# Loading a corner of the query weights with sixteen small loads on few DMA engines, in an attention decode kernel

## The chip, the cores and the metric

The kernel runs on one core of a Trainium2 chip. The core has a matrix engine (TensorE, PE in the profile), a vector engine (VectorE, DVE), an activation engine (ScalarE, ACT), a general engine (GpSimd, POOL), a queue engine that here only issues loads and the store (SyncE, SP), and 16 DMA engines that move data between the chip's memory and the core's on-chip memory of 128 partitions. The metric is the device time of one execution in microseconds, as the median of several runs. Lower is better.

## What is computed

One token of attention for 32 sequences: a query projection, attention over the last 512 positions of a key and value cache with 8 key heads shared by 32 query heads, and an output projection. Everything is bf16.

```
x: [32, 1, 512]   k_cache, v_cache: [32, 8, 2048, 128]
wq: [512, 4096]   wo: [4096, 512]     W = 512, rep = 4
q = (x @ wq).reshape(B, Sq, 32, 128).transpose(0, 2, 1, 3)
k = repeat(k_cache[:, :, Sk - W:, :], rep, axis=1)
v = repeat(v_cache[:, :, Sk - W:, :], rep, axis=1)
p = softmax(einsum("bhqd,bhkd->bhqk", q, k) * Dh ** -0.5)
o = einsum("bhqk,bhkd->bhqd", p, v)
out = o.transpose(0, 2, 1, 3).reshape(B, Sq, 4096) @ wo
```

The windows of the two caches are 33.6 MB each, wq and wo 4.2 MB each.

## The kernel before

**Start.** ACT issues four small loads of x, with 2, 6, 10 and 14 of its 32 rows (`X_PARTS`, L187). SP issues two loads of wq. Row 4p + k of wq goes to partition p, slice k (k = 0 to 3), so that a partition's four rows are contiguous in memory; load 0 brings slices 0 and 1, load 1 slices 2 and 3, 16 KB in each partition each time (`load_wq`, L193). Load 0 is issued before the block of engine programs, load 1 is the first instruction of SP's program. They use the buffer `V_sb[1]`, which later holds values.

**Query projection.** PE transposes x with four matmuls into the PSUM bank `Y_ps` (L301), DVE casts the result into `xT_sb` (L413). Then PE runs, for each slice k and each of eight column groups n of 512 columns, one matmul of `xT_sb[:, k]` with the slice's columns into PSUM bank n (L313): 32 matmuls, accumulated over k. When slice 3 is done for a group, the semaphore `pe_q` goes up. DVE copies the even groups and ACT the odd ones into `Q_row` (L434, L490). DVE transposes that into `QT_sb` (L437), and POOL spreads it into the block-diagonal `QBD`.

**The loop.** Eight steps q take four sequences each. For each, K and V are loaded into one of two buffers (4 MB a load; the V loads of steps 5, 6 and 7 come in two halves), DVE transposes K in two halves (`turn`, T, L445), PE computes scores (S, L331), ACT exponentiates, DVE normalizes, PE moves the probabilities to the layout of the value rows (E, L346), ACT and DVE spread them into the buffer `bd` (B), and PE multiplies them by V (P, L361). The results are picked out of PSUM (C), folded by matmuls with an identity (F, L373) and put away in `o_sel` (D). PE's, DVE's and ACT's orders of these operations are written out by hand at the top of the file, as is SP's order of loads:

```
K0 K1 V0.0 K2 V1.0 K3 V2.0 K4 V3.0 K5 K6 V4.0 K7 V5.0 V5.1 V6.0 V6.1 V7.0 V7.1 W0 W1 W2
```

SP issues a K load (L228) once DVE has transposed what is in the buffer, a V load (L236) once PE has consumed it (V1 waits for `pe_q` at 8, since it overwrites wq), and the three pieces of wo (W0, W1, W2: 2048, 1536 and 512 KB, L242) once the last but one K is transposed; they go into the K buffer.

**End.** PE multiplies `o_sel` with each piece of wo as it lands (L393), DVE and ACT copy the result out of PSUM in two steps, and SP stores it (L248).

**A buffer with two lives.** `bd` holds two halves. The first use of its half 0 is the spreading of step 0; its half 1 also holds x, the identities and `xT_sb` at the start.

Of the kernel before, what the change touches and what calls it, by code (L numbers as in the profile page):

```python
# [6 lines left out]
F32 = mybir.dt.float32  # L7
ACTF = mybir.ActivationFunctionType
# [30 lines left out]
X_PARTS = [(0, 2), (2, 8), (8, 18), (18, 32)]  # L39
V_PIECES = [1, 1, 1, 1, 1, 2, 2, 2]  # L40
WOP = [(0, 16), (16, 28), (28, 32)]


def ops_of(text):
# [3 lines left out]
def bass_standalone__sliding_block_cached__sampling_kernel(  # L48
# [10 lines left out]
    HD = wq.shape[1]  # L59
# [60 lines left out]
    with ExitStack() as es:  # L120
# [23 lines left out]
        junk = sb("junk", [P, 2], F32)  # L144

        wq_sb = V_sb[1][:, :].rearrange("p (kt n) -> p kt n", kt=DKT)
        wo_sb = K_sb[0][:, :].rearrange("p (i n) -> p i n", i=NI)


# [11 lines left out]

        ps = es.enter_context(nc.psum_tensor("ps", [P, 8, 512], F32))
        S_ps, EP_ps, O_ps, F_ps, Y_ps = ps[:, 0], ps[:, 1], ps[:, 2:6], ps[:, 6], ps[:, 7]

        sem_x = sem("sem_x")
        sem_wq = [sem(f"sem_wq{i}") for i in range(DKT // 2)]
        sem_k = [sem(f"sem_k{i}") for i in range(2)]
        sem_v = [[sem(f"sem_v{i}_{j}") for j in range(max(V_PIECES))] for i in range(2)]
        sem_wo = [sem(f"sem_wo{i}") for i in range(len(WOP))]
        sem_out = sem("sem_out")  # L170
        names = (
            "pe_xT pe_q pe_Y dve_xT dve_q dve_QT dve_m dve_r dve_y dve_c act_q act_y act_warm "
            "pool_x pool_e pool_ei pool_q pool_f pool_m pool_j pool_qbd pool_fz"
        ).split()
        s = {n: sem(n) for n in names}
# [14 lines left out]

        def load_wq(i):

            nc.sync.dma_start(  # L193
                wq_sb[:, 2 * i:2 * i + 2, :].rearrange("p k n -> p (k n)"),
                wq.rearrange("(p k) n -> p k n", k=DKT)[:, 2 * i:2 * i + 2].rearrange("p k n -> p (k n)"),
            ).then_inc(sem_wq[i], 16)

        load_wq(0)
# [19 lines left out]
        @block.sync  # L218
        def _(sp):
            wait = Waits(sp)  # L220
            load_wq(1)
            wo_r = wo.rearrange("(p i) n -> p i n", i=NI)
            for op in ops_of(" ".join(LOADS)):
                kind, q = op[0], op[1]
                if kind == "K":
                    if q >= 2:
                        wait([ends["T", q - 2, 1]])
                    sp.dma_start(K_sb[q % 2][:, :], rows(k_cache, q)).then_inc(sem_k[q % 2], 16)  # L228
                elif kind == "V":
                    if q == 1:  # L230
                        sp.wait_ge(s["pe_q"], 8)
                    if q >= 2:
                        wait([ends["P", q - 2, 31]])
                    n = R // V_PIECES[q]
                    r0 = op[2] * n
                    sp.dma_start(  # L236
                        V_sb[q % 2][:, r0 * DH:(r0 + n) * DH], rows(v_cache, q, r0, r0 + n)
                    ).then_inc(sem_v[q % 2][op[2]], 16)
                else:
                    wait([ends["T", NQ - 2, 1]])  # L240
                    i0, i1 = WOP[q]
                    sp.dma_start(  # L242
                        wo_sb[:, i0:i1, :].rearrange("p i n -> p (i n)"),
                        wo_r[:, i0:i1, :].rearrange("p i n -> p (i n)"),
                    ).then_inc(sem_wo[q], 16)
            sp.wait_ge(s["dve_y"], 2)
            sp.wait_ge(s["act_y"], 2)
            sp.dma_start(  # L248
                out.rearrange("b s n -> b (s n)"), out_sb[:, :, :].rearrange("b c n -> b (c n)")
            ).then_inc(sem_out, 16)  # L250
            sp.wait_ge(sem_out, 16)
# [44 lines left out]
        def _(pe):  # L296
# [3 lines left out]
            for kt in range(DKT):  # L300
# [4 lines left out]
                    start=True, stop=True, tile_position=(0, 0),  # L305
                )
            ins.then_inc(s["pe_xT"], 1)
            pe.wait_ge(s["dve_xT"], 1)
            for kt in range(DKT):
                if kt % 2 == 0:  # L310
                    pe.wait_ge(sem_wq[kt // 2], 16)
                for n in range(8):
                    ins = pe.matmul(  # L313
                        ps[:, n], lhsT=xT_sb[:, kt, :], rhs=wq_sb[:, kt, n * 512:(n + 1) * 512],
                        start=kt == 0, stop=kt == DKT - 1, tile_position=(0, 0),
                    )
                    if kt == DKT - 1:
                        ins.then_inc(s["pe_q"], 1)

            def scores(q, w):  # L320
                if w == 0:
# [87 lines left out]
        @block.vector  # L409
        def _(dve):  # L410
            wait = Waits(dve)
            dve.wait_ge(s["pe_xT"], 1)
            dve.tensor_copy(  # L413
                xT_sb[:, :, :].rearrange("p k c -> p (k c)"), Y_ps
            ).then_inc(s["dve_xT"], 1)
            dve.wait_ge(s["pool_f"], 2)
            dve.tensor_reduce(
                F_hd[:, :], F_id[:, :, :].rearrange("p r h -> p h r"), AX.X, ALU.add
            ).then_inc(s["dve_c"], 1)
            dve.wait_ge(s["pool_m"], 2)  # L420
            dve.tensor_reduce(
                m_red[:, :].rearrange("p (h k) -> p h k", h=HKV),
                m_id[:, :, :, :].rearrange("p b h k -> p h k b"), AX.X, ALU.add,
            ).then_inc(s["dve_c"], 1)
            dve.wait_ge(s["dve_c"], 2)
            dve.wait_ge(s["pool_fz"], 1)
            dve.tensor_reduce(
                mask[:, :], m_red[:, :].rearrange("p (h k) -> p h k", h=HKV), AX.X, ALU.add
            ).then_inc(s["dve_c"], 1)
            for d in range(4):  # L430
                dve.tensor_copy(F_sb[:, d, :, d], F_hd[:, :]).then_inc(s["dve_c"], 1)
            for n in range(4):
                dve.wait_ge(s["pe_q"], 2 * n + 1)
                dve.tensor_copy(Q_row[:, 1024 * n:1024 * n + 512], ps[:, 2 * n]).then_inc(s["dve_q"], 1)  # L434
            dve.wait_ge(s["dve_q"], 4)
            dve.wait_ge(s["act_q"], 4)
            dve.transpose(  # L437
                QT_sb[:, :, :, :, :].bitcast(F32).rearrange("p j w h t -> p h w (j t)"),
                Q_row.bitcast(F32).rearrange("p (h w c) -> p h w c", h=HQ, w=2),
            ).then_inc(s["dve_QT"], 1)  # L440
            dve.wait_ge(s["dve_QT"], 1)

            def turn(q, w):
                dve.wait_ge(sem_k[q % 2], 16 * (q // 2 + 1))
                return dve.transpose(  # L445
                    KT_sb[:, w].bitcast(F32).rearrange("p r c t -> p r (c t)"),
                    K_sb[q % 2][:, :].bitcast(F32).rearrange("p (r w c) -> p r w c", r=R, w=2)[:, :, w],
                )

            def maxes(q):  # L450
                dve.tensor_reduce(maxv[:, q:q + 1], S_ps, AX.X, ALU.max).then_inc(s["dve_m"], 1)  # L451
                dve.wait_ge(s["dve_m"], q + 1)
                return dve.tensor_scalar(  # L453
                    negmax[:, q:q + 1], maxv[:, q:q + 1], -SCALE, None, op0=ALU.mult)

            def norm(q):
                dve.reciprocal(recip[:, q:q + 1], sums[:, q:q + 1]).then_inc(s["dve_r"], 1)
                dve.wait_ge(s["dve_r"], q + 1)
                return dve.tensor_scalar(  # L459
                    P_bf[:, :], P_f32[:, :], recip[:, q:q + 1], None, op0=ALU.mult)  # L460

            def spread(q, h0, h1):
                for h in range(h0, h1):
                    o, i, m = spread_args(q, h)
                    ins = dve.tensor_scalar(o, i, m, None, op0=ALU.mult)  # L465
                return ins

            def pick(q, r0, r1):
                for r in range(r0, r1):
                    ins = dve.tensor_copy(*pick_args(q, r))  # L470
                return ins

            run = {"T": turn, "M": maxes, "N": norm, "B": spread, "C": pick}
            for op in orders["DVE"]:
                wait(needs(op))
                run[op[0]](*op[1:]).then_inc(op_sem["DVE", op[0]], 1)
            for c in (0, 2):
                dve.wait_ge(s["pe_Y"], c // 2 + 1)
                dve.tensor_copy(  # L479
                    out_sb[:, c, :], Y_ps[32 * c:32 * (c + 1), 0:P]  # L480
                ).then_inc(s["dve_y"], 1)

        @block.scalar
        def _(act):
            wait = Waits(act)
            act.wait_ge(s["pool_j"], 1)
            act.activation(junk[:, 1:2], junk[:, 0:1], ACTF.Exp).then_inc(s["act_warm"], 1)
            for n in range(4):
                act.wait_ge(s["pe_q"], 2 * n + 2)
                act.activation(  # L490
                    Q_row[:, 1024 * n + 512:1024 * n + 1024], ps[:, 2 * n + 1], ACTF.Copy
                ).then_inc(s["act_q"], 1)
# [66 lines left out]
```

## Time and profile before

| what | value |
|---|---|
| time, median of 3 runs | 186.34 us (186.14 to 186.37) |
| the profiled execution's own time | 186.56 us |
| its span, first to last instruction | 184.7 us |
| mean granted TensorE clock | 0.823 |
| PE, DVE, ACT, POOL busy | 65%, 58%, 27%, 9% of the span |
| DMA: bytes, mean rate | 75.80 MB, 410 GB/s |
| share of the chain of waits that is DMA | 77% |
| issue of the K0 load by SP | 1.65 us |
| x transposes on PE (L301) | from 9.20 us |
| wq matmuls on PE (L313), 32 of them | from 10.57 us, 8.51 us |
| Q transpose on DVE (L437) | 20.13 us, 3.62 us |
| first K transposes on DVE (L445) | from 23.78 us |
| last wo load issued / last PE work on it | 157.99 / 181.68 us |

The span is shorter than the time by what lies before the first and behind the last instruction. Times inside the execution are counted from the span's start. A load's landing is told by a semaphore that each DMA engine involved raises once its share has arrived, so the trace holds up to 16 landing events for a load. The trace also holds a record of every packet that a DMA engine moved, with its queue (q1 is SP's, q10 is ACT's, q8 and q14 bring instructions), start, duration and size, but not the number of the engine.

### The profile page before, as it was taken

Reading aid. Unit: us, or ns where it says so; the run is one execution under the profiler, and the core shown is the slowest. Engines: PE = TensorE matmul, PEld = TensorE weight load, DVE = VectorE, ACT = ScalarE, POOL = GpSimd, SP = SyncE. Lnnn points to the kernel's source line nnn. Section 1 sums busy time; section 2 is a strip of 40 time slices with the busy share of each in tenths; the row PEclk is TensorE's granted clock in tenths of the full one; section 3 lists DMA queues with packets and bytes.
Section 4 is the critical chain, followed back from the end, with each engine's and each line's share of the span. In section 5 each row is a group of like instructions: output and inputs, shape, how many; then the busy total and the mean of one; then the engine's idle time right before and its main releaser. Section 6 shows DMA issues by size and latency. Waiting matters only on the chain.

```text
span 184.7 us, 3662 instructions
## 1 busy us (share of the span) xinstructions
PE 119.1 (65%) x1636; PEld 56.8 (31%) x1636; DVE 106.6 (58%) x106; ACT 49.8 (27%) x93; POOL 16.9 (9%) x52
## 2 busy tenths in 40 slices
PE   0089104447696795549944992441799899888872
PEld 0034000014452351304431350000345445444362
DVE  0031999994549631973299327999646996302031
ACT  3001300011935157001650162001062704502031
POOL 7900040202000200002000200020000000000000
PEclk9999955555599999657987699555579999999999
DMA  6999999999999999999999999999999999999970
GB/s 217 415 490 390 426 454 454 433 390 426 451 447 429 405 422 447 440 436 397 421 451 447 433 397 426 447 440 426 419 429 405 426 426 422 440 412 429 423 299 30
DMA packets 3584, 75.80 MB, mean 410 GB/s; under 512 B 432, under 2 KB 496, under 8 KB 624
## 3 DMA queue, kind: packets, MB, share of 16 engines
q1 hardware_dynamic: 3504, 75.53, 95.9%
q8 instruction: 13, 0.21, 0.5%
q10 hardware_dynamic: 64, 0.03, 0.1%
q14 instruction: 3, 0.02, 0.0%
HBM read 75.53 MB, written 0.03 MB: 409 GB/s over the span
## 4 chain that ended last, share of the span: by engine, by line
DMA 77%; DVE 13%; issue 3%; PE 3%; SPq 3%; DVEq 0%
DMA K_sb<-in_k_cache_dram 49%; DMA V_sb<-in_v_cache_dram 15%; DMA K_sb<-in_wo_dram 13%; DVE KT_sb L445 12%; PE ps L361 2%; SPq L236 1%; SPq L228 1%; SPq L242 1%; PE ps L331 1%; SPq L193 0%; DVE C_sb L470 0%; DVE maxv L451 0%; PE ps L393 0%; DVEq L120 0%; DVE P_bf L479 0%
## 5 line engine op out<-in xcount | busy, mean ns | idle before, releaser
L445 DVE STREAM_TRANSPOSE KT_sb<-K_sb 128x4096 f32<-128x4096 f32 x16 | 70.6, 4433 | 12.5 <-DMA K_sb<-in_k_cache_dram 12.4
L361 PE MATMUL ps<-V_sb,bd 32*128 32x512 bf16 x1024 | 63.1, 397 | 4.7 <-DMA V_sb<-in_v_cache_dram 2.9
L331 PE MATMUL ps<-KT_sb,QBD 128*32 128x512 bf16 x256 | 25.3, 532 | 39.7 <-DVE KT_sb L445 30.0
L361 PEld LDWEIGHTS ps<-V_sb,bd 32*128 32x128 bf16 x1024 | 27.0, 97 | 38.1 <-issue 12.3
L331 PEld LDWEIGHTS ps<-KT_sb,QBD 128*32 128x32 bf16 x256 | 6.6, 114 | 56.1 <-DVE KT_sb L445 37.0
L496 ACT ACTIVATE P_f<-ps,negmax 128x512 f32<-128x512 f32 x8 | 5.5, 687 | 63.1 <-DVE negmax L453 63.1
L509 ACT ACTIVATE bd<-PTc,mask 128x512 bf16<-128x512 bf16 x31 | 20.1, 710 | 0.3
L514 ACT ACTIVATE C_sb<-ps 32x512 f32<-32x512 f32 x22 | 12.9, 587 | 25.6 <-PE ps L361 25.4
L289 POOL COPY QBD<-QT_sb 32x128 bf16<-32x128 bf16 x32 | 9.2, 287 | 106.6 <-PE ps L331 90.2
L465 DVE TENSOR_SCALAR bd<-PTc,mask 128x512 bf16<-128x512 bf16 x33 | 9.3, 348 | 13.8 <-ACT PTc L503 13.8
L470 DVE COPY C_sb<-ps 32x512 f32<-32x512 f32 x10 | 6.9, 693 | 15.7 <-PE ps L361 15.6
L373 PE MATMUL ps<-C_sb,F_sb 128*128 128x128 f32 x64 | 10.0, 303 | 6.3 <-ACT C_sb L514 5.7
L346 PE MATMUL ps<-P_bf,E_sb 128*128 128x128 bf16 x128 | 11.0, 255 | 0.8 <-DVE P_bf L459 0.8
L373 PEld LDWEIGHTS ps<-C_sb,F_sb 128*128 128x128 f32 x64 | 8.3, 203 | 9.3 <-ACT C_sb L514 8.0
L346 PEld LDWEIGHTS ps<-P_bf,E_sb 128*128 128x128 bf16 x128 | 9.3, 116 | 4.9 <-DVE P_bf L459 2.8
L451 DVE TENSOR_REDUCE maxv<-ps 128x1 f32<-128x512 f32 x8 | 5.5, 686 | 7.3 <-PE ps L331 7.2
L503 ACT ACTIVATE PTc<-ps 128x512 bf16<-128x512 f32 x8 | 4.8, 594 | 18.2 <-PE ps L346 18.0
L313 PE MATMUL ps<-V_sb,bd 128*128 128x512 bf16 x32 | 8.5, 433 | 0.8 <-DVE bd L413 0.8
L301 PE MATMUL ps<-bd 32*128 32x128 bf16 x4 | 0.6, 296 | 9.2 <-DMA bd<-in_x_dram 9.2
L413 DVE CAST bd<-ps 128x512 bf16<-128x512 f32 x1 | 0.7, 692 | 9.8 <-PE ps L301 9.8
L434 DVE CAST KT_sb<-ps 128x512 bf16<-128x512 f32 x4 | 2.5, 684 | 6.0 <-PE ps L313 6.0
L490 ACT ACTIVATE KT_sb<-ps 128x512 bf16<-128x512 f32 x4 | 2.1, 603 | 14.0 <-PE ps L313 14.0
(29 smaller groups left out, 33.9 us busy)
## 6 DMA issues: line engine op xcount, KB each, us to landing
K_sb<-in_k_cache_dram SPq DMA_DIRECT2D x8, 4096.0 KB, 25.7
V_sb<-in_v_cache_dram SPq DMA_DIRECT2D x5, 4096.0 KB, 30.1
V_sb<-in_v_cache_dram SPq DMA_DIRECT2D x6, 2048.0 KB, 16.5
V_sb<-in_wq_dram SPq DMA_DIRECT2D x2, 2048.0 KB, 10.0
K_sb<-in_wo_dram SPq DMA_DIRECT2D x1, 2048.0 KB, 19.9
K_sb<-in_wo_dram SPq DMA_DIRECT2D x1, 1536.0 KB, 22.9
K_sb<-in_wo_dram SPq DMA_DIRECT2D x1, 512.0 KB, 23.6
out_dram<-P_bf SPq DMA_DIRECT2D x1, 32.0 KB, 1.5
```

What stands on the lines that cost most here:

```text
L289: pool.tensor_copy(QBD[pr, q % 2].rearrange("p (w t) (h c) -> p w t h c", w=2, h=HKV)[:, :, :, :, 4 * b:4 * b + 4], QT_sb[pr, q].rearrange ...
L313: ins = pe.matmul(ps[:, n], lhsT=xT_sb[:, kt, :], rhs=wq_sb[:, kt, n * 512:(n + 1) * 512], start=kt == 0, stop=kt == DKT - 1, tile_positio ...
L331: ins = pe.matmul(S_ps[32 * c:32 * c + 32, :], lhsT=QBD[:, q % 2, 2 * w + t, c0:c0 + 32], rhs=KT_sb[:, w, :, KB * h:KB * h + KB, t], start ...
L346: ins = pe.matmul(EP_ps[:, e * R:(e + 1) * R], lhsT=E_sb[:, k, e].rearrange("p m j -> p (m j)"), rhs=P_bf[:, k * R:(k + 1) * R], start=k = ...
L361: ins = pe.matmul(O_ps[:, b, :], lhsT=bd[pr, q % 2, 4 * g:4 * g + 4].rearrange("p r h e -> p (r h e)"), rhs=V_sb[q % 2][pr, 512 * g:512 * ...
L373: ins = pe.matmul(F_ps[:, 0:P], lhsT=F_sb[:, d].rearrange("p h d -> p (h d)"), rhs=C_sb[:, q % 2, :, 32 * d:32 * d + 32], start=d == 0, st ...
L445: return dve.transpose(KT_sb[:, w].bitcast(F32).rearrange("p r c t -> p r (c t)"), K_sb[q % 2][:, :].bitcast(F32).rearrange("p (r w c) -> ...
L451: dve.tensor_reduce(maxv[:, q:q + 1], S_ps, AX.X, ALU.max).then_inc(s["dve_m"], 1)
L465: ins = dve.tensor_scalar(o, i, m, None, op0=ALU.mult)
L470: ins = dve.tensor_copy(*pick_args(q, r))
L509: ins = act.activation(o, i, ACTF.Copy, scale=m)
L514: ins = act.activation(*pick_args(q, r), ACTF.Copy)
```

## The change

The second wq load brings slice 2 in full and only the first 3072 columns of slice 3: 14 KB in each partition instead of 16. The cut-off corner, 1024 columns of the 128 rows 4j + 3, is loaded by 16 new loads. Each takes rows of 2 KB, one or two for each of e partitions (e = 3, 5 or 6, four partitions apart), into 48 partitions of half 0 of `bd`, in three slots. Four loads have e = 3 (one row each, j from 0), four e = 5 (one row, j from 12), eight e = 6 (two rows, j from 32 and 56). SP issues them behind the second wq load and ahead of K0, after it has waited for a DVE memset that clears the area (rows of the slots that no load fills must be zero).

The x columns that belong to these rows are transposed separately: six more small matmuls on PE behind the four, copied by DVE (two copies, slots 0 and 1) and ACT (two copies, slot 2) into `xTx_sb`, also in `bd`. They use parts of PSUM banks 5 and 6, so PE waits for the ACT copies before group 5 of slice 0 and for the DVE copies before group 6. In slice 3, PE runs groups 0 to 5 as before; groups 6 and 7 are closed by three matmuls each, one for each slot over 64 partitions, after a wait for all 16 loads.

```diff
+WQX = [(0, 3, 32, 1), (12, 5, 0, 1), (32, 6, 0, 2), (56, 6, 32, 2)]
+WQX_AT = {3: (0,), 5: (12,), 6: (32, 56)}
+NX = 6
...
         def load_wq(i):

+            n = 2 * HD - i * (HD - 512 * NX)
             nc.sync.dma_start(
-                wq_sb[:, 2 * i:2 * i + 2, :].rearrange("p k n -> p (k n)"),
-                wq.rearrange("(p k) n -> p k n", k=DKT)[:, 2 * i:2 * i + 2].rearrange("p k n -> p (k n)"),
+                wq_sb[:, 2 * i:2 * i + 2, :].rearrange("p k n -> p (k n)")[:, 0:n],
+                wq.rearrange("(p k) n -> p k n", k=DKT)[:, 2 * i:2 * i + 2].rearrange(
+                    "p k n -> p (k n)")[:, 0:n],
             ).then_inc(sem_wq[i], 16)
...
             load_wq(1)
+            sp.wait_ge(s["dve_wqx"], 1)
+
+            for j0, e, p0, slots in WQX:
+                t = 4 * e * len(WQX_AT[e])
+                rows_x = wq.rearrange("(j k) n -> j k n", k=DKT)[
+                    WQX_AT[e][0]:WQX_AT[e][0] + t * slots, DKT - 1, 512 * NX:].rearrange(
+                        "(s t) n -> t s n", t=t)
+                for r in range(4):
+                    j = j0 - WQX_AT[e][0] + r
+                    s0 = 0 if slots == 2 else 2
+                    sp.dma_start(
+                        wqx_sb[p0 + r:p0 + r + 4 * e - 3:4, s0:s0 + slots, :], rows_x[j:j + 4 * e - 3:4]
+                    ).then_inc(sem_wqx, 16)
...
             ins.then_inc(s["pe_xT"], 1)
+            x_last = x_sb.rearrange("b (j k) -> b k j", k=DKT)[:, DKT - 1]
+            for j0, e, p0, slots in WQX:
+                for i in range(slots):
+                    slot = i if slots == 2 else 2
+                    ins = pe.matmul(
+                        XT_ps[slot][p0:p0 + 4 * e],
+                        lhsT=x_last[:, j0 + 48 * i:j0 + 48 * i + 4 * e],
+                        rhs=xsel[:, :, :].rearrange("p a j -> p (a j)"),
+                        start=True, stop=True, tile_position=(0, p0),
+                    )
+            ins.then_inc(s["pe_xTx"], 1)
...
-                for n in range(8):
+                for n in range(8 if kt < DKT - 1 else NX):
+                    if kt == 0 and n == NX - 1:
+                        pe.wait_ge(s["act_xT"], 2)
+                    if kt == 0 and n == NX:
+                        pe.wait_ge(s["dve_xT"], 3)
...
+            pe.wait_ge(sem_wqx, 16 * 4 * len(WQX))
+            for n in range(NX, 8):
+                for slot in range(3):
+                    ins = pe.matmul(
+                        ps[:, n], lhsT=xTx_sb[:, slot, :],
+                        rhs=wqx_sb[:, slot, (n - NX) * 512:(n - NX + 1) * 512],
+                        start=False, stop=slot == 2, tile_position=(0, 0),
+                    )
+                ins.then_inc(s["pe_q"], 1)
...
         def _(dve):
             wait = Waits(dve)
+            dve.memset(
+                bd[0:64, 0].rearrange("p r h e -> p (r h e)")[:, 0:3456].bitcast(F32), 0.0
+            ).then_inc(s["dve_wqx"], 1)
...
+            dve.wait_ge(s["pe_xTx"], 1)
+            dve.wait_ge(s["dve_wqx"], 1)
+            for j0, e, p0, slots in WQX[2:]:
+                dve.tensor_copy(
+                    xTx_sb[p0:p0 + 4 * e, 0:2, :].rearrange("p s c -> p (s c)"),
+                    XT_ps01[p0:p0 + 4 * e],
+                ).then_inc(s["dve_xT"], 1)
...
+            act.wait_ge(s["dve_wqx"], 1)
+            act.wait_ge(s["pe_xTx"], 1)
+            for j0, e, p0, slots in WQX[:2]:
+                act.activation(
+                    xTx_sb[p0:p0 + 4 * e, 2, :], XT_ps[2][p0:p0 + 4 * e], ACTF.Copy
+                ).then_inc(s["act_xT"], 1)
```

More of the change, by code (lines that the diff above doesn't have):

```diff
@@ L146, in bass_standalone__sliding_block_cached__sampling_kernel @@
         wq_sb = V_sb[1][:, :].rearrange("p (kt n) -> p kt n", kt=DKT)
+        wqx_sb = bd[0:64, 0].rearrange("p r h e -> p (r h e)")[:, 0:3072].rearrange(
+            "p (s n) -> p s n", s=3)
+        xTx_sb = bd[0:64, 0].rearrange("p r h e -> p (r h e)")[:, 3072:3456].rearrange(
+            "p (s c) -> p s c", s=3)
         wo_sb = K_sb[0][:, :].rearrange("p (i n) -> p i n", i=NI)
@@ L163, in bass_standalone__sliding_block_cached__sampling_kernel @@
         S_ps, EP_ps, O_ps, F_ps, Y_ps = ps[:, 0], ps[:, 1], ps[:, 2:6], ps[:, 6], ps[:, 7]
+        XT_ps = [ps[0:64, 6, 0:P], ps[0:64, 6, P:2 * P], ps[0:64, 5, 0:P]]
+        XT_ps01 = ps[0:64, 6, 0:2 * P]
         sem_x = sem("sem_x")
         sem_wq = [sem(f"sem_wq{i}") for i in range(DKT // 2)]
+        sem_wqx = sem("sem_wqx")
         sem_k = [sem(f"sem_k{i}") for i in range(2)]
@@ L171, in bass_standalone__sliding_block_cached__sampling_kernel @@
         names = (
-            "pe_xT pe_q pe_Y dve_xT dve_q dve_QT dve_m dve_r dve_y dve_c act_q act_y act_warm "
+            "pe_xT pe_xTx pe_q pe_Y dve_wqx dve_xT dve_q dve_QT dve_m dve_r dve_y dve_c act_xT act_q act_y act_warm "
             "pool_x pool_e pool_ei pool_q pool_f pool_m pool_j pool_qbd pool_fz"
```

## The prediction

> **What bounds the kernel now.** I read the page first (busy shares, the DMA row, the queues), then the DMA share by stage, then the chain of waits at its end, and last the DMA records one by one. Queues and one stage (45 to 175 us; the last two columns are the share of 16 DMA engines in use and GB/s):
>
> ```profile
> ## 3 DMA queue, kind: packets, MB, share of 16 engines
> q1 hardware_dynamic: 3504, 75.53, 95.9%
> q8 instruction: 13, 0.21, 0.5%
> q10 hardware_dynamic: 64, 0.03, 0.1%
> q14 instruction: 3, 0.02, 0.0%
> ```
> ```profile
> 45.00:175.00 130.00, 96.74 (x1384) 46.69 (x1385) 77.40 (x81) 43.25 (x79) 5.27 (x19) 0.83 1.00 429
> 175.00:184.70 9.70, 5.09 (x156) 3.79 (x148) 1.95 (x4) 2.27 (x6) 0.00 (x0) 0.97 0.44 177
> ```
> No compute engine is full, the DMA engines are. The chain of waits ends in a load of wo that had been queued for 23.64 us:
>
> ```profile
> 157.52 0.43 SPq L242
> 157.95 0.04 issue
> 157.99 23.64 DMA K_sb<-in_wo_dram
> 181.64 0.04 issue
> 181.68 0.42 PE ps L393 x15
> 182.10 0.02 issue
> 182.12 0.28 DVE P_bf L479
> 182.40 0.32 DVEq L120
> ```
> So the end is set by whichever DMA engine finishes its share of wo last, plus a fixed 3.0 us of output (184.7 − 181.64).
>
> **The engines do not finish together.** The last wo load (W2) has 16 landing events, one per engine: 178.3, 178.4, 178.5, 178.5, 178.6, 178.9, 179.1, 179.3, 179.8, 179.9, 180.0, 180.2, 181.3, 181.3, 181.6, 181.6 us. To see which engine is which I followed the packet records: on one engine the next packet starts 3 or 4 ns before the last one ends, which leaves one predecessor for 3237 packets between 5 and 177.5 us and two for 82 (41 ties; most resolved by counting eight packets to a load). A 16 KB packet takes 611 ns, a 32 KB one 1213 to 1224, the same on all. What separates the chains is the instruction fetches. Each of q8's 13 fetches of 16 KB sits on one chain, takes 1.02 to 1.22 us and lengthens the packet behind it by about 0.5: 1.3 to 1.5 us per fetch. They go round eight chains, A to H, then start again: A to D are hit twice (46.6/151.4, 57.6/161.3, 68.2/167.6, 81.5/177.1 us) and end their data at 181.1, 181.2, 180.8, 180.9; E to H once, ending at 179.5, 179.5, 179.3, 179.7; three others took a q14 fetch (178.5 to 178.9); five none (177.8 to 178.2). A landing comes 0.4 us after the data.
>
> **Which of them are the lowest six?** The x loads number them. They have 2, 6, 10 and 14 rows, and after the first, six chains carry three rows (the lowest six engines), four carry two (engines 6 to 9), four one (10 to 13), two none. The late ones: A and B carry two rows, C one: not among the six. H carries three: among them. G carries none. D and E tie with another chain to the nanosecond and may carry three or one. In the order of the fetches the rows are A 2, B 2, C 1, D ?, E ?, F 0 or 1, G 0, H 3: a rising walk over the engines that starts again at H fits with D and E at one, and no such walk fits with D at three. I take D as outside the six with 3 chances in 4.
>
> **What the change moves.** All packets of the second wq load shrink from 16384 to 14336 B. No row shows that size; between 12288 B (460 ns) and 16384 (611) a line gives 535, so 8 packets save 8 x 76 = **0.61 us on every engine** (bounds 0 and 1.2). The 128 cut-off rows of 2 KB come back as 24 rows on engines 0 to 2 (4 + 4 + 16), 20 on engines 3 and 4, 16 on engine 5, with 16, 12 and 8 semaphore packets of about 6 ns net (9 less the overlap). A 2 KB packet is bounded by 46 ns (x rows, 1 KB) and 159 (4 KB of W2); a line gives 84, less 3 overlap: 81. Engines 0 to 2: 24 x 0.081 + 0.10 − 0.61 = **+1.4 us** (bounds +0.5 and +3.2); 3 and 4: 20 x 0.081 + 0.07 − 0.61 = **+1.1**; 5: 16 x 0.081 + 0.05 − 0.61 = **+0.7**. Bytes in total stay the same.
>
> End of data then: B 181.2 − 0.6 = 180.6, A 180.5, D 180.3 if outside; H 179.7 + 0.7 = 180.4 as engine 5, 180.8 as 3 or 4, 181.1 as 0 to 2; q14 chains at most 178.9 + 1.4 = 180.3; clean low ones 179.6. The last moves from 181.2 to 180.6 (or 180.8): **−0.4 to −0.6, I take −0.5**. What is late next is H, level with B.
>
> **The costs around it.** SP's issues sit between the second wq load (ends 1.60) and K0 (1.65):
>
> ```profile
> 0.73 0.87 SPq L193 DMA_DIRECT2D V_sb<-in_wq_dram  x2
> 0.74 1.60 ACTq L187 DMA_DIRECT2D bd<-in_x_dram  x4
> 1.65 1.25 SPq L228 DMA_DIRECT2D K_sb<-in_k_cache_dram  x2
> ```
> First comes a wait for a DVE memset of 64x1728 f32. No DVE memset is shown; POOL's 128x512 f32 took 0.52, which scales to 1.76; DVE's own 128x512 f32 copy (0.69) to 2.3; a quarter of POOL's is the lower bound. I take 1.8 from 0.7: done at 2.5. Then 16 issues: the single x issues were 0.28 (6 rows), 0.31 (10), 0.38 (14), SP's K loads 0.53 to 0.62 with 0.04 between. By the nearest, 0.33 + 0.03 each: 5.8 us, K0 issued at 8.3. Queued behind them are all K and V loads. The first wq packet started 1.03 us after its issue began (0.73 to 1.76), so K0 flows from 9.3, while the ten upper engines have wq until 12.3 − 0.6 = 11.7: hidden by 2.4 us. At the upper bound (2.3 + 16 x 0.65) K0 flows at 14.4 and those engines idle some 2.3 to 2.7 us.
>
> PE: six small transposes behind the four of L301 (0.58 for four, so 0.9), beside the DVE cast it waits for anyway (0.69 + 0.10): nearly nothing. Then, of the 32 column matmuls two go and six come: 4 x 0.266 (8.51/32) = 1.1 us before Q. The wait for the new rows is met at about 12.2 + 2.0 + 0.4 = 14.6, before PE gets there (18.6). DVE's and ACT's two small copies each lie ahead of banks 5 and 6's turn. Q's 1.1 us pass to the K transposes:
>
> ```profile
> 20.13 3.62 DVE L437 STREAM_TRANSPOSE QT_sb<-KT_sb 128x2048 f32<-128x2048 f32 x1
> 23.78 8.77 DVE L445 STREAM_TRANSPOSE KT_sb<-K_sb 128x4096 f32<-128x4096 f32 x2
> 32.87 4.45 DVE L445 STREAM_TRANSPOSE KT_sb<-K_sb 128x4096 f32<-128x4096 f32 x1 [0.32 <-DMA K_sb<-in_k_cache_dram]
> ```
> The K2 load, issued at 32.58 when they free the buffer, goes out at 33.7; V0 in front of it lands at 41.9 to 42.5, so the queue has 8 us of cover. Without that cover the 1.1 us would be on the end. PE's 23 or so new instructions bring its fetches forward by a tenth of a block, on the same chains.
>
> **Sum.** −0.5 against the profiled execution's 186.56 us (span 184.7); its end before is the same one that the median of 186.34 shows within 0.22. 186.34 − 0.5 = **185.8 us**.
>
> [...]
>
> **Rivals.**
> (1) *A twice-hit chain is among the six* (D). It then ends at 180.9 + 0.7 to 1.4 = 181.6 to 182.3 instead of 181.2: **slower, 186.8 to 187.5**. It decides as soon as D is any of engines 0 to 5. For it: the tie. Against: the walk. 0.23.
> (2) *SP is late with K0*, so the upper engines run dry and lose what they gained: from 0.51 us per small issue on (2.5 + 16 x 0.51 + 1.03 = 11.7). At the bound, 186.3 − 0.6 + 2.5 = 188.2; at 0.58, 186.8. The x issues speak against it. 0.07.
> (3) *The low engines get too much*: H is engine 0 to 2 (181.1), or a 2 KB packet costs 115 ns and more. Then 186.0 to 186.3. 0.12.
> (4) *The loads are spread over all 16 engines*: nothing moves, 186.3. The x loads speak against it. 0.02.
> (5) *A load holds its engines for a fixed time*, of the size of its issue or more: at 0.4 us for each of 16 loads engines 0 to 2 gain 6.4 − 0.6 us and end at 178.0 + 5.8 = 183.8, 189 us. The x loads' rows took 46 ns and their semaphores 9, with the next packet on their heels: 0.01.
> [...]
>
> **Numbers.** The forecast itself (185.65 to 185.97) has 0.55. About 0.2% (0.37 us) can be told from no change here. Faster 0.55 (the forecast), within 0.2% 0.17 ((3), (4), and the near end of (1) and (2)), slower 0.28. Range 185.6 to 187.3: it takes in (3), (4) and most of (1); what is left out is the far end of (1) and of (2).
>
> **What would show it.** The q1 packets of 2 KB should take near 81 ns and lie on six chains; the second wq load should land about 0.6 us earlier; K0's issue should start near 8.3 us; W2's 16 landings should close from 178.3–181.6 to about 178.5–181.0, with the latest two still those that carry two x rows. The forecast is wrong if the last W2 landing belongs to a chain that carried 2 KB packets, or if the upper chains show a gap ahead of K0.

## The result and the profile after

The changed kernel takes **190.85 us** (median of 5 runs, 190.8 to 191.0) against 186.37 (186.14 to 186.53) before: 1.0242 of the time before, interval 1.0227 to 1.0257. The forecast was 185.8, with a range of 185.6 to 187.3. It was wrong in sign and outside its range.

The page of the changed kernel, in the lines that answer to those shown of before. The row DMA is the busy share of the DMA engines in 40 slices of the span, in tenths:

```profile
span 188.9 us, 3705 instructions
...
DMA  6957999999999999999999999999999999999970
...
q1 hardware_dynamic: 3712, 75.53, 94.1%
q8 instruction: 13, 0.21, 0.5%
q10 hardware_dynamic: 64, 0.03, 0.1%
q14 instruction: 4, 0.02, 0.0%
```

The same row before:

```profile
DMA  6999999999999999999999999999999999999970
```

The bytes are those of before (75.53 MB), but q1's share fell from 95.9% to 94.1%, and there is a dent in the third and fourth slice, about 9 to 19 us. The stages of both kernels place it; first before, then after (the last two columns are the DMA share and GB/s):

```profile
12.00:16.00 4.00, 4.00 (x17) 1.63 (x15) 0.00 (x0) 0.00 (x0) 0.00 (x0) 1.00 1.01 434
```
```profile
12.00:16.00 4.00, 4.00 (x12) 1.51 (x11) 0.31 (x4) 0.00 (x0) 0.00 (x0) 1.00 0.19 60
16.00:27.00 11.00, 4.82 (x22) 1.86 (x20) 6.13 (x5) 2.17 (x4) 1.43 (x5) 0.78 1.06 429
45.00:175.00 130.00, 98.79 (x1348) 46.49 (x1344) 80.16 (x84) 43.29 (x79) 5.77 (x20) 0.80 1.00 427
```

For four microseconds the engines are at a fifth (60 GB/s instead of 434); from 16 us on they are as full as before, and the long stage is unchanged. Nothing later makes the pause good. SP's timeline of the changed kernel says why (start, duration, line, what, how many issues in a row):

```profile
0.73 0.87 SPq L206 DMA_DIRECT2D V_sb<-in_wq_dram  x2
2.68 11.95 SPq L246 DMA_DIRECT2D bd<-in_wq_dram  x16
14.67 1.25 SPq L255 DMA_DIRECT2D K_sb<-in_k_cache_dram  x2
```

The 16 small issues take 11.95 us, and K0 is issued at 14.67 instead of 1.65. The chain of waits of the changed kernel now runs through them, one by one, and at its end shows the same wait for wo, only later:

```profile
2.68 0.87 SPq L246
...
13.92 0.71 SPq L246
...
14.67 0.61 SPq L255
...
162.21 23.67 DMA K_sb<-in_wo_dram
185.88 0.04 issue
185.92 0.42 PE ps L444 x15
```

By the packet records the second wq load ended on the 16 engines at 11.63 to 12.13 us (before: 12.32 to 12.75), and K0's first packets started at 16.06 to 17.01 instead of at once (12.32 to 12.75 before). Fifteen of these 16 packets took 1.50 to 2.15 us instead of the usual 1.21. K0 landed at 26.8 to 27.3 (before 22.5 to 23.1) and W2 at 182.5 to 185.9 (before 178.3 to 181.6): some 4.3 us later at both ends of the kernel. The two profiled executions differ by the same 4.26 us (190.82 against 186.56), the medians by 4.48.

### The profile page after: what moved, and what is told of

Its sections match the earlier page's. It is cut to its first block, busy times and chain, and to the rows that moved or that the text cites. A ratio compares the mean times of both kernels' runs of the same rounds, so it can differ in the third digit from the quotient of the medians.

```text
span 188.9 us, 3705 instructions
## 1 busy us (share of the span) xinstructions
PE 124.3 (66%) x1646; PEld 57.8 (31%) x1646; DVE 109.0 (58%) x109; ACT 50.5 (27%) x95; POOL 17.0 (9%) x52
## 3 DMA queue, kind: packets, MB, share of 16 engines
q1 hardware_dynamic: 3712, 75.53, 94.1%
HBM read 75.53 MB, written 0.03 MB: 400 GB/s over the span
## 4 chain that ended last, share of the span: by engine, by line
DMA 66%; DVE 14%; SPq 7%; issue 6%; PE 5%; DVEq 0%
DMA K_sb<-in_k_cache_dram 54%; DMA K_sb<-in_wo_dram 13%; DVE KT_sb L506 12%; SPq L246 6%; PE ps L412 4%; DVE C_sb L531 1%; DVE bd L463 1%; SPq L263 1%; SPq L269 1%; PE ps L382 1%; SPq L255 0%; DVE maxv L512 0%; PE ps L444 0%; DVEq L125 0%; DVE P_bf L540 0%
## 5 line engine op out<-in xcount | busy, mean ns | idle before, releaser
L412 PE MATMUL ps<-V_sb,bd 32*128 32x512 bf16 x1024 | 65.5, 407 | 4.5 <-DMA V_sb<-in_v_cache_dram 2.7
L382 PE MATMUL ps<-KT_sb,QBD 128*32 128x512 bf16 x256 | 26.0, 545 | 38.9 <-DVE KT_sb L506 28.6
L382 PEld LDWEIGHTS ps<-KT_sb,QBD 128*32 128x32 bf16 x256 | 6.7, 115 | 55.6 <-DVE KT_sb L506 35.8
L355 PE MATMUL ps<-V_sb,bd 128*128 128x512 bf16 x30 | 9.1, 476 | 0.4 <-DVE bd L467 0.4
L355 PEld LDWEIGHTS ps<-V_sb,bd 128*128 128x128 bf16 x30 | 3.5, 119 | 5.7 <-issue 3.2
```

The source lines that it names most:

```text
L355: ins = pe.matmul(ps[:, n], lhsT=xT_sb[:, kt, :], rhs=wq_sb[:, kt, n * 512:(n + 1) * 512], start=kt == 0, stop=kt == DKT - 1, tile_positio ...
L382: ins = pe.matmul(S_ps[32 * c:32 * c + 32, :], lhsT=QBD[:, q % 2, 2 * w + t, c0:c0 + 32], rhs=KT_sb[:, w, :, KB * h:KB * h + KB, t], start ...
L412: ins = pe.matmul(O_ps[:, b, :], lhsT=bd[pr, q % 2, 4 * g:4 * g + 4].rearrange("p r h e -> p (r h e)"), rhs=V_sb[q % 2][pr, 512 * g:512 * ...
```

## The experiments

All ratios are to the kernel before, run beside them on the same chip (medians 186.38 to 186.44). A diff marked "to after" starts from the changed kernel, one marked "to before" from the kernel before.

**k0_first.** To after: the loop of 16 small loads, with its wait, is moved behind the issue of K0.

```diff
             load_wq(1)
-            sp.wait_ge(s["dve_wqx"], 1)
-            for j0, e, p0, slots in WQX:
...
                     sp.dma_start(K_sb[q % 2][:, :], rows(k_cache, q)).then_inc(sem_k[q % 2], 16)
+                    if q == 0:
+                        sp.wait_ge(s["dve_wqx"], 1)
+                        for j0, e, p0, slots in WQX:
...
```

> The changed kernel with one move: SP issues K0 right behind the second wq load, and only then waits for the memset and issues the 16 small loads. Theory S (SP needs about 0.75 us for each small load, K0 waits behind them, and all 16 DMA engines run dry until K0 flows at 16.1 us; nothing else of the change costs): the gap is gone, upper engines gain 0.6 us, time 185.7 to 186.3. The new rows now land behind K0 on the low engines (about 24.5 us), Q is ready about 5 us later, and K2 is issued at about 40 us with V0 still flowing until 41.5, so the cover is thin; if it breaks, 186.5 to 187. Rival W (the extra work costs: 2 KB packets on the low engines, more matmuls before Q): still 189 or more.

Measured: 188.19 us (188.02 to 189.15), ratio 1.0097 (1.0077 to 1.0117). The first pause is gone: K0 landed at 21.9 to 22.3, 0.6 us ahead of before, and its first packets took 1.21 us. But SP's timeline shows a second one being made:

```profile
1.64 0.63 SPq L242 DMA_DIRECT2D K_sb<-in_k_cache_dram  x1
2.68 11.94 SPq L254 DMA_DIRECT2D bd<-in_wq_dram  x16
14.66 0.59 SPq L242 DMA_DIRECT2D K_sb<-in_k_cache_dram  x1
15.30 0.60 SPq L264 DMA_DIRECT2D V_sb<-in_v_cache_dram  x1
40.96 0.54 SPq L242 DMA_DIRECT2D K_sb<-in_k_cache_dram  x1
```

The small rows now land behind K0, at 25.0, so Q is late (its transpose starts at 28.52 instead of 20.13), the K transposes start at 32.16, and K2 is issued at 40.96 instead of 32.58. The upper engines had finished V0 at 41.3, before K2's packets came; K2 landed at 53.4 to 55.6 (before 51.6 to 53.5). Removing the first pause gives back 2.7 of the 4.5 us; the second pause keeps the rest, since K0 lands 0.6 to 0.8 us ahead of before and K2 1.8 to 2.1 us behind it. The 8 us of cover that the prediction gave to K2 were used up.

**merged4.** To after: the same rows in four loads of 12, 20, 24 and 24 adjacent partitions.

```diff
-                for r in range(4):
-                    j = j0 - WQX_AT[e][0] + r
...
+                sp.dma_start(
+                    wqx_sb[p0:p0 + 4 * e, s0:s0 + slots, :], rows_x[j:j + 4 * e]
+                ).then_inc(sem_wqx, 16)
...
```

> [...] Theory S: SP's issues take 4 x 0.75 = 3 us, K0 is issued near 5.7 us and flows behind wq without a gap; engines 0 to 9 carry 11 rows (11 x 0.081 + 0.03 - 0.61 = +0.3 us), engines 12 to 15 lose 0.6; the last engine of before (it carried two x rows, so it is one of 6 to 9) ends 0.3 later: 186.5 to 186.8. Rival W: the work is the same, so 189 or more.

Measured: 187.72 us (187.65 to 187.80), ratio 1.0066 (1.005 to 1.0082).

```profile
2.68 1.51 SPq L245 DMA_DIRECT2D bd<-in_wq_dram  x4
4.23 1.25 SPq L254 DMA_DIRECT2D K_sb<-in_k_cache_dram  x2
```

K0 goes out at 4.23 and no engine pauses; that part was right. On how many engines each of these loads lay, and so the 11 rows on engines 0 to 9, no run shows. The time is a microsecond above what was expected: the 2 KB packets took 154 ns in the median (84 in the changed kernel), K0's first packets 1.5 to 2.1 us though K0 had been issued 7.4 us before wq ended, and W2 landed at 179.6 to 182.8.

**loads_only.** To before: the memset, the wait, the 16 loads and PE's wait for them, while both wq loads stay whole and nothing uses the small rows.

```diff
+            sp.wait_ge(s["dve_wqx"], 1)
+            for j0, e, p0, slots in WQX:
...
+            pe.wait_ge(sem_wqx, 16 * 4 * len(WQX))
...
```

> The kernel before, plus the DVE memset, SP's wait for it, the 16 small loads in the place they have in the changed kernel, and PE's wait for them ahead of the first scores; the second wq load stays whole and no matmul uses the small loads' data (they are loaded for nothing). Theory S: K0 is issued at 14.7 and flows at 16.1 as in the changed kernel, and since every engine starts again there, the end is the same: 190.6 to 191.0. Rival W: without the extra matmuls and copies most of the loss is gone, 187 to 188.

Measured: 190.93 us (190.77 to 190.97), ratio 1.0235 (1.0219 to 1.0252), with SP's row as in the changed kernel (2.68, 11.93 us, K0 at 14.65). The loads, with their memset and waits, make the whole loss. The rest of PE's, DVE's and ACT's new work adds nothing that can be seen. The second wq load is whole here, and yet the time is the same: behind the pause all engines start K0 together (its 16 landings lie between 26.7 and 27.4 us; 26.8 and 27.3 in the changed kernel), so what an engine had gained or lost before it no longer counted.

**eight.** To after: the 128 rows are regrouped with a fourth slot, so that eight loads carry them, still four partitions apart (the copies and closing matmuls follow).

```diff
-WQX = [(0, 3, 32, 1), (12, 5, 0, 1), (32, 6, 0, 2), (56, 6, 32, 2)]
+WQX = [(0, 6, 32, 2), (48, 5, 0, 4)]
...
```

> The changed kernel with the same 128 rows in 8 loads instead of 16: four of six partitions by two slots, four of five partitions by four slots (so 24 rows on engines 0 to 4 and 8 on engine 5), still ahead of K0, with one slot more in memset, transposes and closing matmuls. Theory S: 8 x 0.75 = 6 us of issues from about 2.9, K0 issued at 9 and flowing at 10.4, before the upper engines end wq at 11.7: no gap. Then the balance of the engines decides, as forecast: 185.7 to 186.0 if none of the six low engines is among those hit by two instruction fetches, 186.8 to 187.5 if one is. Rival W: 189 or more, as the work is the same or a little more.

Measured: 186.58 us (186.41 to 186.73), ratio 1.0005 (0.9996 to 1.0013).

```profile
3.02 6.33 SPq L242 DMA_DIRECT2D bd<-in_wq_dram  x8
9.39 1.25 SPq L251 DMA_DIRECT2D K_sb<-in_k_cache_dram  x2
```

Half the issues, at about the same price each (0.79 us with the gap), bring 4.3 us back. The gain doesn't come: twelve of K0's 16 first packets took 1.34 to 2.26 us, and W2 landed at 178.7 to 181.6, its latest share as before. Summed over K0's packets, that is 0.43 us on each engine above 1.213 us a packet.

**probe.** To before: pairs of small loads of unused rows, in eight forms, behind V0. One run: 189.77 us against 186.43.

```diff
...
+                        for r in range(2):
+                            sp.dma_start(probe[24 + 6 * r:30 + 6 * r, 2, :], w0[0:6]).then_inc(sem_probe, 16)
...
+                        for r in range(2):
+                            sp.dma_start(probe[48 + 6 * r:54 + 6 * r, 2, :], w0[0:21:4]).then_inc(sem_probe, 16)
+                        for r in range(2):
+                            sp.dma_start(probe[64 + r:64 + r + 21:4, 2, :], w0[0:6]).then_inc(sem_probe, 16)
...
```

> The kernel before with 16 extra small loads on SP behind V0 (3.6 us), where nothing waits for SP until 32 us; their data is used by nothing, and step 0's spreading waits for them. Eight forms, two loads each, all of 2 KB rows of wq: 128 partitions; 12, 6 and 3 adjacent partitions from adjacent rows; 6 adjacent partitions from every fourth row; 6 partitions four apart from adjacent rows; 6 partitions four apart from every fourth row (the changed kernel's form with one slot); 6 adjacent partitions by two slots. Theory P (the step between partitions makes an issue long): 0.30 to 0.40 us for the adjacent forms, 0.65 to 0.75 for both forms four apart. Rival E (few engines make it long): 0.65 to 0.75 for all forms of 6 and 3, 0.33 for 12. Rival D (the number of dimensions, or the step in memory): long where rows step by four or where there are two slots.

The rows of SP's timeline, each for two loads. In order: 128 partitions; 12 adjacent; 6 adjacent; 3 adjacent; 6 adjacent from every fourth row of memory; 6 partitions four apart from adjacent rows; four apart from every fourth row; 6 adjacent with two rows each:

```profile
3.60 1.10 SPq L244 DMA_DIRECT2D bd<-in_wq_dram  x2
4.74 0.83 SPq L246 DMA_DIRECT2D bd<-in_wq_dram  x2
5.62 0.65 SPq L248 DMA_DIRECT2D bd<-in_wq_dram  x2
6.31 0.65 SPq L250 DMA_DIRECT2D bd<-in_wq_dram  x2
7.00 0.63 SPq L252 DMA_DIRECT2D bd<-in_wq_dram  x2
7.67 1.55 SPq L254 DMA_DIRECT2D bd<-in_wq_dram  x2
9.26 1.36 SPq L256 DMA_DIRECT2D bd<-in_wq_dram  x2
10.67 5.70 SPq L258 DMA_DIRECT2D bd<-in_wq_dram  x2
```

Three or six adjacent partitions cost 0.27 to 0.31 us each, whether the rows of memory are adjacent or not. The same six rows written four partitions apart cost 0.66 to 0.79. So it is the step between the partitions written (theory P), not the number of engines (E) and not the step in memory (D). The pairs four apart also came later in the queue than the adjacent ones; step1, next, shows 16 adjacent loads in a row at 0.24 to 0.33 us, so the place in the queue isn't it either. The last pair took 2.06 and 3.59 us and says nothing of its form: in k0_first two-row loads went out as usual. What held SP there is not shown: 17 loads were issued ahead of them from K0 on, but in k0_first it issued K1 and V0 at 0.6 us each behind 17 loads, so their number alone isn't it.

**step1.** To after: each load's partitions and rows are adjacent; the rows, engines and slots stay.

```diff
-                    j = j0 - WQX_AT[e][0] + r
+                    j = j0 - WQX_AT[e][0] + r * e
...
-                        wqx_sb[p0 + r:p0 + r + 4 * e - 3:4, s0:s0 + slots, :], rows_x[j:j + 4 * e - 3:4]
+                        wqx_sb[p0 + r * e:p0 + r * e + e, s0:s0 + slots, :], rows_x[j:j + e]
```

> The changed kernel with the same 16 loads of 3, 5 and 6 partitions in the same slots on the same engines, but each load's partitions and rows are adjacent rather than four apart (partition p of a slot still holds the same row). Theory P: 16 x 0.36 = 5.8 us, K0 issued at 8.5 and ahead of the end of wq, so at most the first K0 packets are late: 186.0 to 187.0. Rival E (few engines make the issue long): K0 at 14.6 as in the changed kernel, 190.6 to 191.

```profile
2.68 5.38 SPq L246 DMA_DIRECT2D bd<-in_wq_dram  x16
8.10 1.25 SPq L255 DMA_DIRECT2D K_sb<-in_k_cache_dram  x2
```

The issue price is 0.336 us, gaps included, and K0 goes out at 8.10: this is the prediction's SP row (5.8 us, K0 at 8.3), reached by the one edit. The pause is gone. The time, however, is 187.35 us (ratio 1.0048, 1.002 to 1.0076), and its 12 runs fall into two groups: six at 186.30 to 186.68, six at 188.03 to 188.68. In the profiled run (186.44) W2 landed at 179.3 to 181.6. The 2 KB packets took 95 ns in the median and 142 or more in the slowest tenth, against 84 and 116 in the changed kernel. K0's packets were slower too: the first of each engine took 1.32 to 1.53 us, the second 1.29 to 1.83, and over the whole load that is 0.54 us on each engine above 1.213 us a packet.

**wait9.** To before: `sp.wait_ge(s["pool_e"], 5)` behind the second wq load, which delays K0 and what SP issues behind it, and changes nothing else.

> The kernel before with nothing added but one wait: SP issues K0 only after POOL's last copy into E_sb, at about 9.1 us, 3.2 us before wq's last packets end. Theory R (a load has to be in the queue about 3 us ahead for its first packets to come without a pause; in the 8-load kernel, with K0 issued at 9.4, the first K0 packets took 1.4 to 2.3 us where 1.21 is usual): the first K0 packets of most engines take 1.6 us or more, and the end moves by 0.3 to 0.9: 186.7 to 187.3. Rival C (the pause comes from the small loads beside it): first packets of 1.21 and 186.3 to 186.5.

Measured: 186.34 us (186.15 to 187.02), ratio 1.0 (0.9991 to 1.0008).

```profile
9.04 1.25 SPq L229 DMA_DIRECT2D K_sb<-in_k_cache_dram  x2
```

K0 issued 7.4 us later (9.04 against 1.65) cost nothing here, where it was in the queue 3.2 us before wq ended; its first packets took 1.21 us but for two. step1 (3.5 us) and merged4 (7.4 us) gave it a longer lead and have the long packets, so there a late issue (R) is not the cause; small loads in the queue ahead of K0 (C) agree. `eight` had a lead of 2.3 us only, so for it R isn't excluded. Why they lengthen only what comes right behind them in that place, and not K1's packets beside them in k0_first, stays open.

**k0_v1.** To k0_first: V1 is issued ahead of K2, to cover the second pause.

```diff
-K0 K1 V0.0 K2 V1.0 K3 V2.0 K4 V3.0 K5 K6 V4.0 K7 V5.0 V5.1 V6.0 V6.1 V7.0 V7.1 W0 W1 W2
+K0 K1 V0.0 V1.0 K2 K3 V2.0 K4 V3.0 K5 K6 V4.0 K7 V5.0 V5.1 V6.0 V6.1 V7.0 V7.1 W0 W1 W2
```

> The changed kernel with K0 ahead of the wait and the 16 loads, and with V1 ahead of K2 in SP's order, so that the queue is not empty while K2 waits for the K transposes that the late Q delays (in the run with K0 first alone, K2 was issued at 40.96 us and the upper engines paused at 42 us). Theory S with that cover: no pause anywhere, upper engines 0.6 us earlier, low ones 0.7 to 1.4 later: 185.7 to 186.0 if none of the twice-hit engines is among the low six, 186.8 to 187.5 if one is. If step 2, which now gets its keys 10 us later, starves a later load instead: above 187.5.

Measured: no pause is left. Of 12 runs four took 185.59 to 185.75, close to the prediction's 185.8, and eight 186.89 to 187.70; the median is 187.07, ratio 1.0009 (0.9984 to 1.0033; the two medians alone would give 1.0034). The profiled run was one of the upper group (187.14), and yet its span is 184.3 and its W2 landed at 178.4 to 181.0, 0.6 us ahead of before, as forecast. PE, in its last stretch, was held up once on its way through the middle piece of wo, without a data wait:

```profile
179.78 0.62 PE L445 MATMUL ps<-K_sb,o_sel 128*32 128x128 bf16 x30 [0.69 <-DMA K_sb<-in_wo_dram]
181.05 0.68 PE L445 MATMUL ps<-K_sb,o_sel 128*32 128x128 bf16 x34 [0.65 <-issue]
```

**v1_shift100, b_shift11, b_shift100.** If that stop was PE's instruction fetch at an unlucky place, moving PE's later instructions by some extra one-column matmuls ahead of the first scores should change the groups. The traces of before and after agree with fetches at places in PE's program: the first of q8's 13 fetches of 16 KB starts behind 240 of PE's matmuls and weight loads before, behind 216 after. v1_shift100 adds 100 of them to k0_v1; the other two add 11 and 100 to the kernel before.

```diff
+                    for _ in range(100):
+                        pe.matmul(
+                            Y_ps[0:32, 0:1], lhsT=QBD[:, 0, 0, 0:32], rhs=QBD[:, 0, 0, 0:1],
+                            start=True, stop=True, tile_position=(0, 0),
+                        )
```

> The kernel with K0 ahead of the 16 loads and V1 ahead of K2, plus 100 matmuls of one column ahead of the first scores (their results are used by nothing), while PE waits for keys anyway, so that PE's later instructions lie some 200 further on in its program. That kernel's times fell into two groups, 185.6 to 185.8 (4 of 12) and 186.9 to 187.7 (8 of 12); its profiled execution, of the second group, shows PE stopping for 0.65 us after 30 of W1's 48 matmuls with nothing to wait for, its last instruction fetch at 186.1 us, behind the span's end at 184.3, and 2.8 us of time outside the span where 1.8 is usual. Theory F (the second group comes from where PE's 16 KB instruction blocks begin: a block begins in the last matmuls and its fetch stands behind data): all runs in one group near 185.6 to 185.9. Rival T (the second group comes from twice-hit chains that are now and then among the low six engines): two groups as before, since the engines' loads are the same.

> The kernel before with 11 such one-column matmuls (22 instructions more, about as many as the change adds to PE) at the same place and nothing else. Theory F: the block boundaries move as in the changed kernel, and a part of the runs goes up by 0.5 to 2 us, a second group at 187 to 188. Rival T: no small loads, no second group: 186.2 to 187.0 as before.

> The kernel before with 100 such matmuls and nothing else, a control for the run of 100 on the other kernel: theory S and the forecast (the gain comes from the wq rows moved to the low engines) expect 186.2 to 186.7 here; if the shift itself brings the gain, 185.6 to 186.0.

Measured: v1_shift100 again has two groups, five runs at 185.64 to 186.22 and seven at 187.15 to 188.13 (median 187.18, ratio 1.0021, 0.9993 to 1.0048). b_shift11 is at 186.41 (186.35 to 186.58; ratio 1.0001), b_shift100 at 186.51 (186.32 to 187.24; 1.001). So the groups don't go when PE's later instructions are moved (F falls as it was put), and moving them alone brings neither a second group nor a gain to the kernel before.

**k0_v1_step1.** To k0_v1: the small loads write adjacent partitions, as in step1.

> This joins the two mends: K0 issued ahead of the 16 small loads with V1 ahead of K2 in the list, and each small load writing adjacent partitions. Theory S: SP is a resource in series, and with K0 ahead nothing waits for the 16 issues, so their price does not matter any more: the lower times stay at 185.6 to 185.8, as without the adjacency, with 16 issues in 5.4 us instead of 11.9 and K1 issued at 8.2 instead of 14.7. Rival X, the upper group of times (about 187) comes from SP being busy with the small loads when K1 should go out: then the upper group disappears here and nearly all runs lie at 185.6 to 185.8. Theory G, the upper group comes from an instruction fetch on one of the six engines or from anything else at the end of the kernel: two groups stay, 185.6 to 185.8 and 186.9 to 188. If the profile falls in the upper group, its last landings of wo tell which: later than 181.1 for an engine that carried 2 KB packets.

```profile
1.64 0.61 SPq L242 DMA_DIRECT2D K_sb<-in_k_cache_dram  x1
2.68 5.48 SPq L254 DMA_DIRECT2D bd<-in_wq_dram  x16
8.21 0.54 SPq L242 DMA_DIRECT2D K_sb<-in_k_cache_dram  x1
```

Measured: 187.51 us, ratio 1.006 (1.0036 to 1.0083): two runs at 186.5, four at 187.33 to 188.05. SP is free 6.5 us sooner, and both groups are there still, so X falls. Even the lower group is 0.8 us above k0_v1's; theory S missed that. The packets give a part of it: the 2 KB packets are at 95 ns in the median and 142 or more in the slowest tenth here, 84 and 85 in k0_v1, 13.6 us against 11.8 in sum, or 0.3 us on each of six engines, if they are shared alike. W2's latest share landed at 181.6 instead of 181.0.

## Why the prediction was wrong, point by point

- **The step that failed** is the sentence "By the nearest, 0.33 + 0.03 each: 5.8 us, K0 issued at 8.3." Sixteen issues took 0.64 to 0.87 us each, 11.95 in all, and K0 went out at 14.67. The nearest row was chosen by number of rows (x loads of 6 to 14), while the price hung on the step between the partitions written: for six rows 0.30 us adjacent and 0.66 to 0.79 four apart in probe, and, gaps included, 0.34 in step1 against 0.75 in the changed kernel. The x loads write adjacent ones. That difference stood in the diff, and no row of before had it, so the 0.65 taken as upper bound, from loads of another form, was no bound. A smaller part came on top: K0's first packet started 1.39 us after its issue (16.06), not 1.03.
- **The rival that came true** is (2), SP late with K0, given 0.07. Its mechanism is the one that the runs show, and the gap ahead of K0 is a sign that the prediction had named. Its threshold of 0.51 us for an issue lies between the two prices that were run, 0.75 with a pause and 0.34 (step1) without one; it was not narrowed further. Its worst case of 188.2 was still too low, for the price and for a second term: after the pause K0's first packets took 0.3 to 0.9 us longer than 1.21. The first of them starts 3.7 us later than before (16.06 against 12.32); with these 0.3 to 0.9 that makes 4.0 to 4.6, and 4.3 was measured.
- **Upper engines −0.61 us**: right. All 128 packets of 14336 B took 535 to 540 ns; the second wq load ended on all engines 0.6 to 0.7 us sooner. In the changed kernel it bought nothing, as all engines started K0 together behind the pause.
- **2 KB packets at 84 ns**: right (median 84, 81 back to back). They lie on six chains: in the changed kernel's trace six of 16 go on from the second wq load to 2 KB packets without a gap, and q1 has 80 packets of 4 B more than before (480 against 400), as three, five or six engines a load make (4 x 3 + 4 x 5 + 8 x 6); in k0_v1's trace ten of K1's 16 landings lie within 0.33 us, the other six 1.74 to 2.59 us behind the first. "The lowest six" and "the upper engines" stand for these six chains and the other ten. The prediction's figures for the rows give a difference of 1.35 to 2.04; rival (5), at 0.4 us for each of 16 loads, would give 6.4 and falls.
- **The memset of 1.8 us, done at 2.5**: 1.50 us, done at 2.66, right in effect.
- **PE and Q**: Q's transpose starts at 21.56, 1.4 us later (1.1 forecast), and is hidden, since K0 lands at 26.8 anyway. loads_only, without that work, takes as long.
- **K2's 8 us of cover** was right for the forecast's own order and is what k0_first used up by moving the small rows behind K0.
- **The sum of −0.5** did not come in the forecast's own order of loads. step1 meets the forecast's issue price and K0's place, and its six lower runs are at 186.30 to 186.68. The prediction put one term at nothing: K0's packets were slower right behind the small loads. This comes to 0.54 us on each engine in step1 (0.59 in merged4, 0.43 in `eight`, 0.02 in k0_v1, where K0 goes first), nearly all of the 0.61 us gained. With K0 first and V1 ahead of K2 a gain is there in a part of the runs, four of 12 in k0_v1 at 185.59 to 185.75 and five of 12 in v1_shift100 at 185.64 to 186.22. How much of it comes from the moved rows is not shown, since the kernel before was not run with V1 ahead of K2.
- **D outside the lowest six**, taken with three chances in four: right in four traces (step1, k0_v1, v1_shift100, k0_v1_step1), if the fetches go round the same eight chains as before. There K1's landings fall into ten early and six late ones, and the first four fetches of q8 each move one of the ten: six early ones are left at 90 us. So the chains that are hit twice are not among the six with 2 KB packets.
- **The two groups of times** were not foreseen. The upper one is about 1.4 to 1.7 us longer, which in size and sign would suit rival (1) if the fetches sat on other chains from run to run; no trace shows that. Of the 25 upper runs of these four kernels, 17 have a span longer by 0.6 to 2.4 us and the usual 1.7 to 2.0 us outside it; eight have 2.4 to 2.9 us outside, which rival (1) doesn't explain. The one trace of such a run (k0_v1) is also the only one of all with an instruction fetch behind the end of its span (186.1 us, span 184.3). A trace of a run with a longer span wasn't taken. The cause stays open.

The issue of such a load was not small beside the load itself: 0.71 us for a two-row load whose packets take 2 x 84 ns on each of its engines. The last of the 16 took 1.87 us in all, from the start of its issue (13.92) to the end of the last small packet (15.79). Loads with neighbouring partitions had slower packets (95 to 154 ns in the median against 84 four apart); no run here shows why.

No version beats the kernel before: `eight` equals it, and k0_v1 and v1_shift100 are ahead of its fastest run (186.14) in eight of their 24 runs only.

## What to carry to other kernels

Every load behind the small ones in SP's queue waited for the sum of their issues (11.95 us for 16, K0 at 14.67 instead of 1.65): multiply the number of new issues by the price of their exact form, and compare the sum with the moment at which the engines behind run dry. Take the price of an issue from a row with the same step between destination partitions, not the same bytes (0.30 against 0.66 to 0.79 us for the same six rows in probe); if there is none, the range has no upper end yet, and the rival that hangs on it deserves more than a few per cent. Look at the big load right behind small ones, too: its packets took about half a microsecond more on each engine here, nearly as much as the change was to gain. When small loads are moved behind a big one, follow what waits for them (here Q, then the K transposes, then K2's issue) before calling them hidden.

## What the runs showed of the hardware

- An issue by SP took 0.24 to 0.35 us for three to six adjacent partitions (probe, step1, k0_v1_step1), and 0.64 to 0.87 for three to six partitions four apart (changed kernel). Neither the step in memory (0.66 against 0.71 and 0.79 in probe) nor a second row for a partition (0.71 against 0.64 to 0.70) changed that much.
- Behind a pause of about 4 us (changed kernel), 15 of the first 16 packets of 32 KB took 1.50 to 2.15 us instead of 1.21; in k0_first the first seven packets of K2, behind a pause of over 1 us and with no small load near, took 1.9 to 2.5. Right behind small loads, without a long pause, they took 1.2 to 2.3 in `eight` (12 of 16 at 1.34 to 2.26), 1.5 to 2.1 in merged4 and 1.3 to 1.5 in step1.
- The 2 KB packets took 84 ns in the median four partitions apart (changed kernel, k0_v1), 95 adjacent (step1, k0_v1_step1; a tenth of them 142 or more), and 154 in four loads of 12 to 24 adjacent partitions (merged4).
- Behind K0, K1, V0 and 14 small loads, SP's next two issues took 2.06 and 3.59 us (probe).
- step1, k0_v1, v1_shift100 and k0_v1_step1 each have two groups of times, 1.4 to 1.7 us apart; the kernel before, `eight` and merged4 have one.
